# Transposing DMAs in one chain, and queries and keys loaded between the output weights

## The chip, the cores and the metric

The kernel runs on one core of a Trainium2 chip. Its time is the device time of one execution in microseconds (us), given as the median of five runs. One execution is also recorded by the hardware profiler; its page and its trace are what this document reads. Five engines work side by side, each through its own list of instructions in order: TensorE (PE; its weight loads are shown as PEld), VectorE (DVE), ScalarE (ACT), GpSimd (POOL) and SyncE (SP). Here POOL does little but issue the loads, and SP issues the transposing DMAs and the stores. The data of all of them move through the same 16 DMA engines.

## What is computed

An attention whose weights are squared ReLUs, not a softmax, and behind it a gated feed-forward block. There are 8 batches, 12 heads, 448 positions and a head dimension of 64; the block goes from 768 to 1536 and back to 768.

```python
def _attn_ref(q, k, v):
    S = q.shape[2]
    scale = 1.0 / np.sqrt(q.shape[-1])
    scores = scale * np.matmul(q, k.transpose(0, 1, 3, 2))
    attn = np.maximum(scores, 0.0) ** 2 / S
    return np.matmul(attn, v).astype(np.float32)

def _moe_ref(x, w_gate, w_val, w_out):
    g = x @ w_gate
    gelu = 0.5 * g * (1.0 + erf(g * inv_sqrt2))
    val = x @ w_val
    return (gelu * val @ w_out).astype(np.float32)
```

The output of the attention, with its heads laid side by side, is the `x` of the block. Inputs and output are float32 in DRAM; the loads convert to bfloat16.

## The kernel before

**Work of one batch.** Queries and keys of a batch are loaded into one tile `qk16` (queries in the lower 64 partitions, keys in the upper), values into `v16`. For the scores, queries and keys must be transposed into `qkT`. For the first two batches TensorE does this against an identity matrix (L342), and DVE copies the result (L346). From batch 2 on (the third) it is done by DMA: DVE rearranges one group of four heads into `qkr` (L258), and SP issues two transposing DMAs for the group (L262), one for four of its seven chunks of positions and one for the other three. There are three such groups `m` in a batch, so six transposing DMAs. Then come, all over the length of the batch, 21 units of scores (`sp`, TensorE), ReLU (`rl`, ACT, L389) and square (`attnT`, DVE, L395), the six pairs of heads of the values product, whose results DVE copies to `xT` (L448), the gate and value products for 12 columns of the block with Gelu (ACT, L498) and the product `uT` (DVE, L503), and the output tiles (`osb`, ACT copy, L555), which SP stores (L560). All matmuls go through one helper, hence L159.

**Order.** The attention of batch b+1 is interleaved with the block of batch b on TensorE. A planner (`run_plan`, L23) sets the order of every engine's instructions when the program is built. Each piece of work is an `Op` with a cost, other pieces that it waits for and a lag. The lists `PE0` (matmuls on the lower rows) and `POOL` stay in the order in which they were written; from the lists `PE1`, `ACT`, `DVE`, `SP` and `IDLE` the planner takes what can start first, looking at the first 48 pieces. `IDLE` is no engine, only a delay. What the planner settles is an order: on the chip each engine follows its own list and waits by semaphores. For loads the planner keeps a running sum of bytes divided by a rate, and takes a load to have landed 2.0 planned us after its turn in that sum. In the first 30 planned us it also fills gaps of TensorE with matmuls on a tile of zeros (`fill`).

**Loads.** POOL issues them in the order in which they are written (from L581): batch 0, then batch 1 among the gate and value weights `wg` and `wv`, then the four parts of the output weights `wo` (`load_wo`, each 384 of its 1536 rows), then queries and keys of batch 2 in three groups of four heads, then batch 2's values. Loads of batches 3 and later are issued as the block of the batch two before proceeds. Output tile t needs all of `wo`, in order of its rows.

**Transposing DMAs.** `add_dma_transposes` (L248) writes down the delay, the copy and the two transposing DMAs of one group. `EARLY` is 2. For batches after it the second DMA of a group waits on SP for the first to have landed, through the list `one` and a manual dependency; the three groups do not wait for one another. Batch 2 has no such wait: its six DMAs are issued as their copies are done. Batch 2's three groups are written down when the main loop reaches batch 2's first scores (L662); those of later batches when their keys' load is written down.

Of the kernel before, what the change touches and what calls it, by code (L numbers as in the profile page):

```python
# [88 lines left out]
def kernel(  # L89
# [16 lines left out]
    B, H, S, D = q.shape  # L106
    P = 64
    SC = S // P
    VC = (SC + 1) // 2
    NPAIR = H // 2  # L110
    NM = NPAIR // 2
# [13 lines left out]
    EARLY = 2  # L125
# [30 lines left out]
    SYNC = mybir.DependencyInfo(mybir.DependencyClass.Sync, mybir.DependencyReason.DATA)  # L156
# [17 lines left out]
    w12_op, wo_op, head_op = {}, {}, {}  # L174
    qk16, v16 = {}, {}

    def load(nbytes, emit, deps=(), cost=0.7, rate=400e3):
        def paced():
            ins = emit()
            for d in deps:  # L180
                tc.add_manual_dep(ins.ins, d.ins.name, SYNC, reason="pace")

        op = Op("POOL", cost, paced, deps)
        arrivals[op] = nbytes / rate
        POOL.append(op)
        return op

    def load_w12(i):
        cols = slice(i * WCH, (i + 1) * WCH)

        def emit(wt, src):
            return nc.gpsimd.dma_start(
                wt[:, :, :], src[:, cols].rearrange("(c p) f -> p c f", p=128))
        w12_op[i] = [load(4 * d_model * WCH, lambda wt=wt, src=src: emit(wt, src))
                     for wt, src in ((wg[i], moe_w_gate), (wv[i], moe_w_val))]

    def load_wo(i):
        rows = slice(i * WOG * 128, (i + 1) * WOG * 128)
        wo_op[i] = load(4 * WOG * 128 * d_model, lambda: nc.gpsimd.dma_start(
            wo[i][:, :, :], moe_w_out[rows, :].rearrange("(c p) f -> p c f", p=128)))  # L200

    def load_qk(b, i, h0, h1, deps=()):

        src = (q, k)[i]

        def tile_of():
            if b not in qk16:
                qk16[b] = qkv.tile([128, H * S // P * D], bf16, name="qk16", tag="qk16")
            return qk16[b][HALF[i], :]

        op = load(4 * (h1 - h0) * S * D, lambda: nc.gpsimd.dma_start(  # L211
            tile_of().rearrange("p (h x) -> p h x", h=H)[:, h0:h1, :],
            src[b, h0:h1].rearrange("h (p c) d -> p h (c d)", c=SC)), deps, rate=400e3 if b else 300e3)
        for pr in range(h0 // 2, h1 // 2):
            head_op[b, pr, i] = op

    def load_v(b, h0, h1, deps=()):

        for i in range(2):
            def emit(i=i):  # L220
                if b not in v16:
                    v16[b] = qkv.tile([128, H, VC, D], bf16, name="v16", tag="v16")
                c0 = i * (SC - VC)
                return nc.gpsimd.dma_start(  # L224
                    v16[b][HALF[i], h0:h1, :, :],
                    v[b, h0:h1].rearrange("h (p c) d -> p h c d", c=SC)[:, :, c0:c0 + VC, :])
            op = load(4 * (h1 - h0) * VC * P * D, emit, deps, rate=400e3 if b else 300e3)
            for pr in range(h0 // 2, h1 // 2):
                head_op[b, pr, 2 + i] = op

    def load_heads(b, h0, h1):
        load_qk(b, 0, h0, h1)
        load_qk(b, 1, h0, h1)
        load_v(b, h0, h1)

    qkT, tr_op = {}, {}

    def qkT_tile(b):
        if b not in qkT:
            qkT[b] = tpool.tile([128, NM * SC * 2, 2 * P], bf16, name="qkT", tag="qkT")  # L240
        return qkT[b]

    def by_group(t):
        return t.rearrange("d (m c r) x -> d m c r x", m=NM, c=SC)

    qkr = {}

    def add_dma_transposes(b, m):  # L248


        wait = Op("IDLE", 2.0 if b == EARLY else 5.0, lambda: None,
                  [head_op[b, pr, i] for pr in (2 * m, 2 * m + 1) for i in range(2)])
        IDLE.append(wait)

        def emit_copy():
            if b not in qkr:
                qkr[b] = lpool.tile([128, NM, SC, 4, D], bf16, name="qkr", tag="qkr")
            nc.vector.tensor_copy(  # L258
                qkr[b][:, m], qk16[b].rearrange("p (h c d) -> p c h d", c=SC, d=D)[:, :, 4 * m:4 * m + 4])

        def emit_transpose(c0, c1):
            ins = nc.sync.dma_start_transpose(  # L262
                by_group(qkT_tile(b))[:, m, c0:c1].rearrange("d c r x -> d (c r) x"),
                qkr[b][:, m, c0:c1].rearrange("p c h d -> p (c h d)"))
            if b > EARLY:

                if c0:
                    tc.add_manual_dep(ins.ins, one[0].ins.name, SYNC, reason="pace")
                one[:] = [ins]

        one = []
        copy = Op("DVE", 0.65, emit_copy, [wait, *tr_op.get((b - 1, m), ())], lag=0.15, prio=3)
        DVE.append(copy)
        tr_op[b, m] = [Op("SP", 0.19 * 2 * (c1 - c0), lambda c0=c0, c1=c1: emit_transpose(c0, c1),
                          [copy, last_s.get(b - 2)], lag=4.5) for c0, c1 in ((0, VC), (VC, SC))]
        if b > EARLY:
            tr_op[b, m][1].deps.append(tr_op[b, m][0])
        SP.extend(tr_op[b, m])


# [199 lines left out]
    def add_gate_value(at, b, fc, g):  # L480
# [28 lines left out]
        if g == 0:  # L509
            done = gel_op[b, fc] = Op("ACT", 0.55, emit_gelu, [ops[1][-1]], lag=0.06, prio=0)  # L510
            ACT.append(done)
        else:
            done = u_op[b, fc] = Op("DVE", 0.54, emit_mult, [gel_op[b, fc], ops[1][-1]],
                                    lag=0.2, prio=0)
            DVE.append(done)
            if b + 2 < B and b:
                if fc % 2 == 0:
                    m, i = divmod(fc // 2, 2)
                    load_qk(b + 2, i, 4 * m, 4 * m + 4, [done])
                    if i:  # L520
                        add_dma_transposes(b + 2, m)
                elif fc > 6:
                    h0 = 2 * (fc - 7)
                    load_v(b + 2, h0, h0 + 4, [done])
# [56 lines left out]
    for h0, h1 in ((0, 2), (2, 4), (4, 8), (8, 12)):  # L581
        load_qk(0, 0, h0, h1)
        load_qk(0, 1, h0, h1)
        if h0 == 0:
            POOL.append(Op("POOL", 0.6, lambda: make_identity(nc, ident)))
        if h0 > 2:
            load_v(0, h0 - 4, h1 - 4)
# [12 lines left out]
    load_w12(4)  # L600
    load_w12(5)
    for i in range(FC // WOG):
        load_wo(i)
    for m in range(NM):
        for i in range(2):
            load_qk(2, i, 4 * m, 4 * m + 4)
    load_v(2, 0, H)
# [51 lines left out]


    for at, _, fn, args in work:
        if fn is add_scores and args == (2, 0):  # L662
            for m in range(NM):
                add_dma_transposes(2, m)
        fn(at, *args)
# [75 lines left out]
```

## Time and profile before

| | us |
|---|---|
| median of 5 runs | 429.5 (428.2 to 431.69) |
| the profiled execution | 431.69 |
| its span, first to last instruction | 429.8 |
| TensorE busy | 420.8 (98%) |
| TensorE weight loads busy | 359.6 (84%) |
| ScalarE busy | 223.7 (52%) |
| VectorE busy | 212.8 (49%) |
| GpSimd busy | 71.5 (17%) |

The mean granted clock of TensorE is 0.993 of full speed. The page cuts the span into 40 equal slices and gives, for each, the busy share of an engine in tenths, with 9 for 90% and more; the DMA row is the mean busy share of the 16 DMA engines in the same way:

```profile
PE   8999999799999999999999999999999999999996
DVE  2876665157644566355643566455643555212201
ACT  4956662176666555555546555555546555322220
PEclk9999999899999999999999999999999999999998
DMA  7999999977984389544975359845884100120034
```

A slice is 10.7 us. A busy TensorE is not TensorE at its peak, because matmuls overlap one another and their ends are modelled; the number of matmuls in a stretch and the granted clock say more. In lists of waits, "issue" is time for which the profile shows nothing that the engine waited for. A line of the timeline has the start in us, the duration of the merged group, the engine, the source line, the operation, what it writes and reads, how many there are, and in brackets the idle time before it.

The DMAs of the stretch around the change, with issue and landing as the trace has them, in us from the start of the span:

| DMA | issued | landed |
|---|---|---|
| `wo`, four parts | 42.90, 45.73, 46.49, 47.24 | 56.76, 59.56, 62.33, 65.14 |
| batch 2, group 0, queries and keys | 48.49, 50.21 | 66.34, 67.45 |
| group 1 | 52.18, 54.17 | 68.54, 69.70 |
| group 2 | 57.05, 59.84 | 71.21, 72.08 |
| batch 2, values | 62.86, 65.43 | 74.06, 78.31 |
| transposing DMAs, group 0 | 69.88, 74.05 | 78.76, 80.34 |
| stores of the first output tile | 72.84, 73.42 | 79.28, 79.75 |
| transposing DMAs, group 1 | 75.44, 78.59 | 82.62, 83.25 |
| transposing DMAs, group 2 | 83.31, 84.66 | 86.93, 91.62 |

The three copies to `qkr` before the transposing DMAs start at 68.72, 73.54 and 74.6 and take 1.08 us each. The first scores of batch 2 start at 84.8.

### The profile page before, as it was taken

The page shows a single profiled execution, that of the slowest core. Times are in us where ns is not written, and L with a number is a line of the kernel's source. Part 1 is how long each engine was busy: PE and PEld are TensorE (multiplying, and loading weights), DVE is VectorE, ACT ScalarE, POOL GpSimd, SP SyncE. Part 2 cuts the span into 40 slices and gives each one's busy share as a digit, 9 for nine tenths or more (in the row PEclk, how much of TensorE's full clock was granted, in tenths as well). Part 3 has the DMA queues.
Part 4 walks back from the last instruction along what each step waited for, and adds up shares of the span by engine and source line. Part 5 has one row for each costly group of instructions (what it writes and reads, how often), then busy time and mean ns, then how long its engine had stood idle before and what let it go on. Part 6 is the DMA issues. An engine that isn't in the chain of part 4 may idle for free.

```text
span 429.8 us, 19589 instructions
## 1 busy us (share of the span) xinstructions
PE 420.8 (98%) x9087; PEld 359.6 (84%) x9090; DVE 212.8 (49%) x347; ACT 223.7 (52%) x320; POOL 71.5 (17%) x116
## 2 busy tenths in 40 slices
PE   8999999799999999999999999999999999999996
PEld 3558768579998888979999978979999988977895
DVE  2876665157644566355643566455643555212201
ACT  4956662176666555555546555555546555322220
POOL 8655420012200122011300023011310000000000
PEclk9999999899999999999999999999999999999998
DMA  7999999977984389544975359845884100120034
GB/s 99 193 199 197 201 209 193 169 77 97 135 122 93 39 104 135 127 82 69 137 109 118 60 72 150 127 80 58 122 148 103 38 4 3 40 76 2 3 76 113
DMA packets 75217, 44.91 MB, mean 104 GB/s; under 512 B 36096, under 2 KB 71680, under 8 KB 75136
## 3 DMA queue, kind: packets, MB, share of 16 engines
q0 software_dynamic: 37088, 24.39, 42.5%
q1 hardware_dynamic: 37888, 19.08, 25.2%
q8 instruction: 71, 1.16, 1.2%
q10 hardware_dynamic: 160, 0.20, 0.1%
q14 instruction: 10, 0.08, 0.1%
HBM read 48.76 MB, written 11.01 MB: 139 GB/s over the span
## 4 chain that ended last, share of the span: by engine, by line
PE 97%; issue 1%; ACT 1%; DVE 0%
PE ff L159 86%; PE sp L159 8%; PE ff L705 1%; PE ff L304 1%; PE ff L342 1%; PE sp L342 1%; ACT rl L389 1%; DVE qkT L346 0%; DVE attnT L395 0%; DVE osb L555 0%; DVE warm L145 0%; DVE table L148 0%
## 5 line engine op out<-in xcount | busy, mean ns | idle before, releaser
L159 PE MATMUL ff<-xT,wg 64*64 64x448 bf16 x2304 | 217.0, 352 | 0.0
L159 PE MATMUL ff<-xT,wv 64*64 64x448 bf16 x2304 | 215.6, 350 | 0.0
L389 ACT ACTIVATE rl<-sp 128x896 bf16<-128x896 f32 x168 | 152.3, 918 | 96.1 <-PE sp L159 78.4
L159 PE MATMUL ff<-wo,uT 64*64 64x384 bf16 (+1 forms) x2736 | 151.7, 320 | 2.7 <-issue 2.5
L159 PEld LDWEIGHTS <-wv 64*64 64x64 bf16 x2304 | 125.2, 107 | 16.7 <-issue 1.3
L159 PEld LDWEIGHTS <-wg 64*64 64x64 bf16 x2304 | 124.9, 107 | 16.6 <-issue 0.5
L395 DVE TENSOR_TENSOR attnT<-rl 128x896 bf16<-128x896 bf16 x168 | 103.8, 622 | 69.8 <-ACT rl L389 68.6
L159 PEld LDWEIGHTS <-uT 64*64 64x64 bf16 x2736 | 126.2, 107 | 8.8 <-issue 3.8
L159 PE MATMUL sp<-qkT 64*64 64x448 bf16 (+1 forms) x768 | 108.7, 328 | 0.8 <-ACT rl L389 0.5
L503 DVE TENSOR_TENSOR uT<-gel,ff 128x448 bf16<-128x448 bf16 x96 | 59.5, 619 | 82.0 <-PE ff L159 73.1
L159 PE MATMUL ff<-attnT,v 64*64 64x448 bf16 (+1 forms) x768 | 86.1, 326 | 0.1
L498 ACT ACTIVATE gel<-ff 128x448 bf16<-128x448 f32 x96 | 52.1, 543 | 52.1 <-PE ff L159 51.1
L159 PEld LDWEIGHTS <-qkT 64*64 64x64 bf16 x768 | 43.6, 106 | 10.0 <-issue 3.3
L555 ACT COPY osb<-ff 128x384 f32<-128x384 f32 x54 | 25.7, 476 | 49.8 <-PE ff L159 47.1
L159 PEld LDWEIGHTS <-v 64*64 64x64 bf16 x768 | 45.8, 107 | 5.6 <-issue 1.2
L448 DVE TENSOR_SCALAR xT<-ff 128x448 bf16<-128x448 f32 x48 | 29.9, 623 | 33.4 <-PE ff L159 33.4
L211 POOL DMA_DIRECT2D qk<-in_q_dram x25 | 15.6, 622 | 130.5 <-DVE uT L503 123.7
L224 POOL DMA_DIRECT2D v<-in_v_dram x44 | 27.3, 628 | 42.8 <-DVE uT L503 32.0
L211 POOL DMA_DIRECT2D qk<-in_k_dram x25 | 15.4, 615 | 63.5 <-DVE uT L503 55.6
L258 DVE COPY qkr<-qk 128x1792 bf16<-128x1792 bf16 x18 | 19.3, 1078 | 0.0
L555 DVE COPY osb<-ff 128x192 f32<-128x192 f32 (+1 forms) x3 | 1.2, 420 | 18.3 <-PE ff L159 18.3
L342 PEld LDWEIGHTS <-qk 128*64 128x64 bf16 x168 | 5.5, 115 | 2.9 <-issue 2.9
(23 smaller groups left out, 42.6 us busy)
## 6 DMA issues: line engine op xcount, KB each, us to landing
out_dram<-osb SPq DMA_DIRECT2D x54, 192.0 KB, 2.7
v<-in_v_dram POOLq DMA_DIRECT2D x42, 128.0 KB, 4.8
qk<-in_q_dram POOLq DMA_DIRECT2D x23, 224.0 KB, 4.3
qk<-in_k_dram POOLq DMA_DIRECT2D x23, 224.0 KB, 5.1
wg<-in_moe_w_gate_dram POOLq DMA_DIRECT2D x6, 384.0 KB, 10.7
wv<-in_moe_w_val_dram POOLq DMA_DIRECT2D x6, 384.0 KB, 11.8
wo<-in_moe_w_out_dram POOLq DMA_DIRECT2D x4, 576.0 KB, 14.9
v<-in_v_dram POOLq DMA_DIRECT2D x2, 384.0 KB, 12.0
```

Source lines behind the costliest of these rows:

```text
L159: return nc.tensor.matmul(o, lhsT, rhs, start=start, stop=stop, tile_position=(P * row, P * col))
L211: op = load(4 * (h1 - h0) * S * D, lambda: nc.gpsimd.dma_start(tile_of().rearrange("p (h x) -> p h x", h=H)[:, h0:h1, :], src[b, h0:h1].re ...
L224: return nc.gpsimd.dma_start(v16[b][HALF[i], h0:h1, :, :], v[b, h0:h1].rearrange("h (p c) d -> p h c d", c=SC)[:, :, c0:c0 + VC, :])
L258: nc.vector.tensor_copy(qkr[b][:, m], qk16[b].rearrange("p (h c d) -> p c h d", c=SC, d=D)[:, :, 4 * m:4 * m + 4])
L304: nc.tensor.matmul(t[:, :], warm[:, 0:128], warm[:, :], start=True, stop=True)
L342: nc.tensor.transpose(t[HALF[j], c, :], src[:, 2 * (2 * m + r) + j, c, :], ident[:, :], tile_position=(0, P * j))
L389: nc.scalar.activation(rl[:, :, :], box[0][:, :, 0:S], AF.Relu)
L395: nc.vector.tensor_tensor(a[:, :, :], box[1][:, :, :], box[1][:, :, :], op=ALU.mult)
L448: nc.vector.tensor_scalar_mul(xT[b][:, pr, :], box[0][:, 0:S], scalar1=out_scale)
L498: nc.scalar.activation(gel[b, fc][:, :], box[0][:, 0:S], AF.Gelu)
L503: u_op[b, fc].ins = nc.vector.tensor_tensor(uT[b][:, fc, :], gel.pop((b, fc))[:, :], box[0][:, 0:S], op=ALU.mult).ins
L555: (nc.vector.tensor_copy if last else nc.scalar.copy)(osb[t][:, cols], box[0][:, 0:N])
```

## The change

There are four edits, in one step.

1. The rate by which the planner counts loads goes from 400e3 to 425e3 bytes per us, for all loads but those of batch 0's queries, keys and values, which keep 300e3. This alters no load, only the planned times and with them the order in which the planner puts instructions.
2. Every transposing DMA waits for the one before it to have landed, over all groups and batches; in the planner each has the one before among what it waits for.
3. The loads of queries and keys of batch 2's first group stand between the second and the third part of `wo`; the other two groups stay behind the fourth.
4. The copies and transposing DMAs of batch 2 are written down when the main loop comes to batch 1's first gate product, no longer at batch 2's first scores.

```diff
-    def load(nbytes, emit, deps=(), cost=0.7, rate=400e3):
+    def load(nbytes, emit, deps=(), cost=0.7, rate=425e3):
...
-            src[b, h0:h1].rearrange("h (p c) d -> p h (c d)", c=SC)), deps, rate=400e3 if b else 300e3)
+            src[b, h0:h1].rearrange("h (p c) d -> p h (c d)", c=SC)), deps, rate=425e3 if b else 300e3)
...
-            op = load(4 * (h1 - h0) * VC * P * D, emit, deps, rate=400e3 if b else 300e3)
+            op = load(4 * (h1 - h0) * VC * P * D, emit, deps, rate=425e3 if b else 300e3)
...
-    qkr = {}
+    qkr, one, turn = {}, [], []
...
-            if b > EARLY:
-
-                if c0:
-                    tc.add_manual_dep(ins.ins, one[0].ins.name, SYNC, reason="pace")
-                one[:] = [ins]
-
-        one = []
+
+            if one:
+                tc.add_manual_dep(ins.ins, one[0].ins.name, SYNC, reason="pace")
+            one[:] = [ins]
+
...
-        if b > EARLY:
-            tr_op[b, m][1].deps.append(tr_op[b, m][0])
+        for op in tr_op[b, m]:
+            op.deps.extend(turn)
+            turn[:] = [op]
...
     for i in range(FC // WOG):
+        if i == 2:
+            load_qk(2, 0, 0, 4)
+            load_qk(2, 1, 0, 4)
         load_wo(i)
-    for m in range(NM):
+    for m in range(1, NM):
         for i in range(2):
             load_qk(2, i, 4 * m, 4 * m + 4)
...
-        if fn is add_scores and args == (2, 0):
+        if fn is add_gate_value and args == (1, 0, 0):
             for m in range(NM):
                 add_dma_transposes(2, m)
```

## The prediction

> **What bounds the kernel now.** I read four views in turn: the chain of waits, the table of stretches, the order of time around the one stretch that is odd, and the DMA queues.
>
> The chain of waits puts the whole span on TensorE, nearly all of it on matmuls (L159):
>
> ```profile
> PE 97%; issue 1%; ACT 1%; DVE 0%
> ```
>
> So only time in which TensorE stands still, or runs at a lower clock, can be gained. The waits of TensorE name one such place, with no releaser:
>
> ```profile
> PE ff L159 <- issue: 2.5, 1, 2.5
> ```
>
> The table of stretches, one microsecond a row, shows where it is (PE busy, PEld, DVE, ACT, POOL, then granted clock, DMA share, GB/s):
>
> ```profile
> 75.00:76.00 1.00, 1.00 (x30) 0.84 (x24) 0.61 (x1) 0.43 (x1) 0.00 (x0) 1.00 1.39 131
> 76.00:77.00 1.00, 0.40 (x10) 0.00 (x0) 0.00 (x0) 0.00 (x0) 0.00 (x0) 1.00 2.37 107
> 77.00:78.00 1.00, 0.00 (x0) 0.00 (x0) 0.00 (x0) 0.00 (x0) 0.00 (x0) 1.00 0.21 14
> 78.00:79.00 1.00, 0.07 (x4) 0.08 (x8) 0.00 (x0) 0.00 (x0) 0.00 (x0) 0.90 0.81 320
> 79.00:80.00 1.00, 1.00 (x14) 0.63 (x18) 0.00 (x0) 0.00 (x0) 0.00 (x0) 0.50 1.18 262
> 80.00:81.00 1.00, 1.00 (x16) 0.85 (x12) 0.00 (x0) 0.00 (x0) 0.00 (x0) 0.50 1.31 298
> 81.00:82.00 1.00, 1.00 (x16) 0.82 (x9) 0.00 (x0) 0.42 (x1) 0.00 (x0) 0.50 1.50 47
> 82.00:83.00 1.00, 1.00 (x24) 0.71 (x21) 0.00 (x0) 0.60 (x2) 0.00 (x0) 0.90 0.33 65
> ```
>
> Every engine stops together, DMA falls to 14 GB/s, and TensorE then works at a clock of 0.50. The order of time shows what goes on beside it:
>
> ```profile
> 74.05 5.92 SPq L262 DMA_TRANSPOSE qkT<-qkr  x3
> ...
> 76.07 0.33 PE L159 MATMUL ff<-wo,uT 64*64 64x384 bf16 x2
> 78.92 0.12 PEld L159 LDWEIGHTS <-uT 64*64 64x64 bf16 x2 [2.93 <-issue]
> 78.92 0.53 PE L159 MATMUL ff<-wo,uT 64*64 64x384 bf16 x2 [2.53 <-issue]
> ```
>
> The matmul at 78.92 continues an output tile whose inputs were all there, so what was missing is the instruction itself. The queues have a row for that:
>
> ```profile
> q8 instruction: 71, 1.16, 1.2%
> ```
>
> 71 packets of 16,384 bytes against TensorE's 18,195 instructions are 256 to a packet. Counted in 256s, TensorE stops at instruction 10.74, and the small gap before 64.89 stands at 8.74, exactly two packets earlier: both are packet borders. In the trace's packet records the fetches between 38 and 69 start 3.3 to 3.8 us after the border that precedes them, take 0.9 to 1.0 and end 1.3 to 1.6 before the next border; 256 instructions last some 6 us. The fetch of 75.05 started 4.2 us after its border, took 2.40 and ended at 77.45, past the border; work resumed 1.47 later. So an end some 1.3 to 1.5 before the border is just in time, and the fetches before it had no more than 0.3 to spare. From 92 on most start within 1 us of the border (2.5 at most) and leave 3 to 5: the load queue no longer fills the DMA engines, of which it alone moved 204 GB/s between 40 and 70. My reading is that a transposing DMA under full loads delayed a fetch that had no slack.
>
> **What the change costs and gains, step by step.** The sum starts from the profiled execution, 431.69 us (span 429.83 and 1.86 around it). It is the slowest of the five; the median is 429.5.
>
> *The stall that may go.* 2.53 us idle, then 3.3 us at half clock (78.9 to 82.2), which lose 1.65. Together 4.2. The actions and copies after it run 4.3 us later against the kernel's own plan than those before it, which agrees. If no fetch meets a transpose any more: minus 4.2. If one still does, 0.
>
> The Trainium skill, Runtime: NRT & Kernel Launch, section Instruction fetch mechanics, says that crossing a 16 KiB border is mostly hidden because dispatch is slower than the refill; by that nothing here is to be gained and the sum would stay at 431.7. The idle 2.53 us on a border is against it. The page TensorE: Matmul & The Clock Gate, section on the HAM clock gate, has the clock drop after an idle window of about 3.4 us; here 2.53 us of idle was enough for 0.50, so the measurement decides. By the page only 2.53 would be gained.
>
> *The reordered loads.* The first queries and keys of the third batch took 1.20 and 1.11 us of the full queue (landings 65.14, 66.34, 67.45). Moved ahead of wo2 and wo3 (the third and fourth part) they land at about 60.7 and 61.9, and wo2 and wo3 2.31 later, at 64.64 and 67.45. The first output tile reaches wo3's rows at about 67.2. That is a wait of 0.3 us; at the least 0, and 0.9 if transposes already hold the engines. I take 0.3, since the transposes' first packets come at about 66.8 (below). All POOL issues stay the same in number (each waits for the one eight before it, as 57.05 does for the landing at 56.76), and the last two value loads still land long before batch 2's values at 95.0.
>
> *The earlier copies.* The new rate makes the plan expect loads earlier. The loads counted at 400e3 before and 425e3 after, the first copy (L258) becomes due 8.4 us earlier in the plan, the other two 3.0 and 3.1. DVE runs in order, so the copy goes to about 62.7, before the multiply at 63.69, ahead of which DVE was idle 0.95; its 1.08 us fit but for 0.1, which TensorE doesn't see. Its data have landed by 61.9. Without that cover DVE would hold the multiplies and squares behind it, 1 us at most. The second copy now stands ahead of the copy of xT at 73.00 (before which DVE idled 3.21), with its keys at 69.70; cover again, until that landing slips past 72.
>
> *The chain.* Each transposing DMA now waits on SP for the one before; behind it wait only the stores of the first output tiles, whose buffers are four deep. Six in a row from about 63.8, at 4.7 us median to landing and 8.9 at most, end by 92 to 100. Batch 2's first scores ran at 84.8 and need two of the six, the third and fourth some 12 us later: hidden at 4.7 each (73), and hidden at 8.9 each by 3 us (81.6). For later batches pairs were already chained, and a neighbour's pair had landed.
>
> *Fetches in the new place.* The first transpose was issued at 69.88 and moved its first packets at 73.0 under full loads; from 63.8 that is 66.8 to 70. The fetch of 68.55 falls inside. The nearest row of one transpose beside loads is the fetch of 87.72: 1.96 instead of 0.95, thus +1.0; the ends are 0 (missed) and 4.2 (the stall before with its clock). The next fetch, near 75, meets the second transpose or the 3 us gap that the chain leaves between landing and next packets: 0 to 4.2 too. I take 1.0 once, for one of the two, with no loss of clock.
>
> Sum: 431.69 - 4.2 + 0.3 + 1.0 = 428.8. This is 0.7 under the median of 429.5, or 0.2%.
>
> **Rivals.**
>
> *The stall goes altogether.* For it: the chain leaves at most one transpose in flight, and the stores between two transposes no longer pile up (store packets of 3072 bytes took up to 1.9 us at 76.3). Against it: the fetch of 75.05 began late when only the first transpose moved data. If the stall costs each run alike, the time is 429.5 - 4.2 + 0.3 = 425.6.
>
> *More fetches stall (slower).* Transposes now overlap full loads from 66.8 to beyond 80 rather than from 73 to 77, so both the fetch of 68.55 and the one near 75 can starve TensorE. It decides as soon as each is later than its slack of 0.3 us. One as before (4.2) and one at 1.5: 431.69 - 4.2 + 0.3 + 5.7 = 433.5. Against it: with transposes in flight after 90 no fetch took over 1.8.
>
> *One stall trades for one stall.* The second fetch or the first simply takes the place of the old one with its clock loss or without: 430.0 to 431.7, no change to speak of. The chain then doesn't do what it says, since a single transpose is enough.
>
> **How the numbers follow.** Short waits in place of the stall 0.32 (own range 427.3 to 430.8); stall gone 0.28; more stalls 0.28; one for one 0.12. Differences within 0.5% (427.4 to 431.6) are about what this kernel's measurement can't tell from no change. Faster: the 0.28 less a tenth, plus an edge of the likeliest, 0.31. Slower: the 0.28 and an edge of the last, 0.30. The rest, 0.39, is the same. The range takes in 425.5, just under the stall gone, and 433.5.
>
> **What would show it.** In the profile after: the row "issue" of TensorE's waits at 2.5 or gone, and where; the granted clock between 64 and 90 below 1.00 or not; the first copy at about 62.7 and the first transposing DMA at 63.8; a wait for wo at 67; transposes one at a time, the last landing by 100. I am wrong if the stall isn't the fetch, if batch 2's scores wait for the chain, or if DVE held by an early copy stops TensorE.

## The result and the profile after

The changed kernel takes 429.68 us, the median of 43 executions (428.78 to 435.56). The kernel before takes 428.2 us, the median of 80 executions (427.0 to 432.24). The ratio is 1.0031, interval 1.0022 to 1.0041: 0.3%, or 1.3 us, slower. That lies inside the 0.5% called no change in the prediction, but the forecast had the sign the other way.

The page of the changed kernel (execution of 429.82 us, span 428.0) shows the clock, the DMA share and the chain of waits:

```profile
PEclk9999999999999999999999999999999999999998
DMA  8999999999985399545975379635983100120034
PE 81%; DMA 15%; POOL 2%; issue 1%; DVE 0%; DVEq 0%; ACT 0%; POOLq 0%
```

The chain was nearly all TensorE before. Now it leaves TensorE for DMAs at two places. One is the last two transposing DMAs of batch 2 (89.28 to 96.14, 1.6% of the span), ahead of which it is on TensorE again. The other is the wait for `wo` at 67.5, and from there it goes into the loads of the start, most of the 15%. That share is no measure of the loss: a kernel below that has no wait at the first place still shows 14%. The places are what to look for, and the waits of TensorE name three candidates (releaser, total, times, longest):

```profile
PE ff L159 <- DMA wo<-in_moe_w_out_dram: 1.0, 1, 1.0
PE ff L159 <- DVE xT L447: 0.9, 1, 0.9
PE ff L159 <- issue: 0.7, 1, 0.7
```

The old wait of 2.5 without a releaser has become three waits of about 1 us with three different causes. The order of time of TensorE places them:

```profile
67.58 0.35 PE L159 MATMUL ff<-wo,uT 64*64 64x384 bf16 x2 [0.95 <-DMA wo<-in_moe_w_out_dram]
...
77.34 0.35 PE L159 MATMUL ff<-wo,uT 64*64 64x384 bf16 x2 [0.68 <-issue]
...
98.12 0.57 PE L159 MATMUL ff<-xT,wg 64*64 64x448 bf16 x6 [0.92 <-DVE xT L447]
```

The first is the fourth part of `wo`, which landed at 67.54. The second stands at instruction 10.74 counted in packets of 256, the same packet border as before. The third is new and far from the loads that were moved. VectorE's order of time shows where it comes from:

```profile
62.17 1.08 DVE L258 COPY qkr<-qk 128x1792 bf16<-128x1792 bf16 x1
...
71.96 1.09 DVE L258 COPY qkr<-qk 128x1792 bf16<-128x1792 bf16 x1 [2.85 <-DMA qk<-in_k_dram]
73.10 0.62 DVE L447 TENSOR_SCALAR xT<-ff 128x448 bf16<-128x448 f32 x1
75.05 1.09 DVE L258 COPY qkr<-qk 128x1792 bf16<-128x1792 bf16 x1 [1.32 <-DMA qk<-in_k_dram]
...
96.45 1.09 DVE L258 COPY qkr<-qk 128x1792 bf16<-128x1792 bf16 x1 [2.08 <-DMA qkT<-qkr]
97.46 0.61 DVE L447 TENSOR_SCALAR xT<-ff 128x448 bf16<-128x448 f32 x1
```

The first three copies are batch 2's, at the places that were forecast. The fourth, at 96.45, is batch 3's first. It writes `qkr`, of which there is one buffer (`lpool`, one tile), so it must wait until batch 2's last transposing DMA has read it; that landed at 96.14. Behind the copy on VectorE stands the copy of `xT`, and TensorE waits for that.

The DMAs of the stretch, in us from the start of the span:

| DMA | issued | landed |
|---|---|---|
| `wo`, four parts | | 56.84, 59.88, 64.74, 67.54 |
| batch 2, group 0, queries and keys | | 60.74, 61.88 |
| groups 1 and 2, keys | | 71.87, 74.96 |
| batch 2, values | 61.27, 62.17 | 77.34, 79.10 |
| transposing DMAs, one to three | 63.34, 74.90, 79.98 | 74.89, 79.90, 83.70 |
| transposing DMAs, four to six | 83.71, 89.28, 92.73 | 89.22, 92.71, 96.14 |

### The profile page after: what moved, and what is told of

It reads as the page before. It is cut to its first block, busy times and chain, and to the rows that moved or that the text cites. A ratio compares the mean times of both kernels' runs of the same rounds, so it can differ in the third digit from the quotient of the medians.

```text
span 428.0 us, 19588 instructions
## 1 busy us (share of the span) xinstructions
PE 419.0 (98%) x9087; PEld 358.2 (84%) x9090; DVE 213.1 (50%) x347; ACT 223.7 (52%) x320; POOL 71.5 (17%) x116
## 4 chain that ended last, share of the span: by engine, by line
PE 81%; DMA 15%; POOL 2%; issue 1%; DVE 0%; DVEq 0%; ACT 0%; POOLq 0%
PE ff L159 75%; PE sp L159 6%; DMA wv<-in_moe_w_val_dram 5%; DMA qk<-in_k_dram 4%; DMA wo<-in_moe_w_out_dram 4%; DMA qkT<-qkr 2%; POOL qk L211 1%; POOL v L224 0%; POOL wg L192 0%; DVE xT L447 0%; DVE osb L554 0%; POOL ident masks.py:199 0%; POOL ident masks.py:197 0%; DVEq L258 0%; DVE qkr L258 0%
## 5 line engine op out<-in xcount | busy, mean ns | idle before, releaser
L211 POOL DMA_DIRECT2D qk<-in_k_dram x25 | 15.4, 615 | 66.6 <-DVE uT L502 57.8
```

## The experiments

All ratios are to the kernel before, timed on the same chip in the same rounds.

**What the old pause costs, and what the planner's rate does alone.** The profiled execution of before (431.69 us) was far above the median, so I took another, unchanged.

> The kernel before, unchanged, for a profile of an ordinary execution, since the one recorded (431.69 us) was far above the median of 428.2. Theory (the recorded one was one of the rare executions in which the pause at the packet border was long enough to lower the clock): the pause near 76 us is 0.3 to 1.5 us, the granted clock stays at 1.00, span about 426.5. Rival (every execution has the pause of 2.5 us and the half clock): span about 429.8 with a clock of 0.50 behind 78 us.

It ran in 428.27 us, span 426.5. Its waits of TensorE:

```profile
PE ff L159 <- issue: 1.2, 1, 1.2
```

The pause is there, at the same packet border (75.70 to 77.17 from the start of one matmul to the start of the next), but it is 1.2 us and not 2.5, and the granted clock stayed at 1.00 behind it. The fetch began 4.32 us after its border and took 0.92. Of the 80 executions of the kernel before, 73 took 429.6 us or less and seven 431.08 or more, none between. The one that the prediction was worked from is of the seven. Another 93 executions of this kernel were timed beside the experiments, each with its mean granted clock: nine took 430.7 us or more, and eight of these had a clock of 0.993 to 0.996, all the others 0.997 or more. So a long execution is as a rule one that lost its clock.

Then edit 1 by itself:

```diff
-    def load(nbytes, emit, deps=(), cost=0.7, rate=400e3):
+    def load(nbytes, emit, deps=(), cost=0.7, rate=425e3):
...
-            src[b, h0:h1].rearrange("h (p c) d -> p h (c d)", c=SC)), deps, rate=400e3 if b else 300e3)
+            src[b, h0:h1].rearrange("h (p c) d -> p h (c d)", c=SC)), deps, rate=425e3 if b else 300e3)
...
-            op = load(4 * (h1 - h0) * VC * P * D, emit, deps, rate=400e3 if b else 300e3)
+            op = load(4 * (h1 - h0) * VC * P * D, emit, deps, rate=425e3 if b else 300e3)
```

> Only the rate of 425e3, nothing else of the change. It puts the copy of batch 3's first group ahead of the xT copy on VectorE, as the changed kernel has it, but the transposes of batch 2 aren't chained. Theory (the order alone is harmless, it needs the late chain): no wait for xT near 97 us, ratio 0.998 to 1.001. Rival (the reordered plan itself costs the time): ratio 1.003 and the wait for xT of about 0.9 us.

Ratio 1.0004 (0.9983 to 1.0025). The pause is 0.9 us. Batch 3's first copy to `qkr` now stands ahead of a copy of `xT` on VectorE. The kernel before, in its ordinary execution:

```profile
94.62 0.62 DVE L448 TENSOR_SCALAR xT<-ff 128x448 bf16<-128x448 f32 x1 [0.41 <-PE ff L159]
95.16 1.08 DVE L258 COPY qkr<-qk 128x1792 bf16<-128x1792 bf16 x1
```

and with the new rate alone:

```profile
93.43 1.08 DVE L258 COPY qkr<-qk 128x1792 bf16<-128x1792 bf16 x1
94.43 0.62 DVE L448 TENSOR_SCALAR xT<-ff 128x448 bf16<-128x448 f32 x1
```

Without the chain nothing holds the copy (batch 2's last transposing DMA landed at 89.45) and TensorE has no wait there. So this edit sets the order, and alone it costs nothing.

**Is the wait for `xT` the loss?** Two kernels take it away in different ways. One gives `qkr` a second buffer:

```diff
-    lpool = ctx.enter_context(tc.tile_pool(name="lpool", bufs=1))
+    lpool = ctx.enter_context(tc.tile_pool(name="lpool", bufs=2))
```

> The changed kernel with two buffers for qkr, so that batch 3's first copy doesn't wait for batch 2's last transpose. Theory (the chain ends at 96.1 us and the copy, which stands ahead of xT's on VectorE, waits for it): the wait for xT of 0.9 us near 97 goes, the waits for wo (1.0) and at the packet border (0.7) stay; some 1.2 us less than the changed kernel, ratio to the kernel before about 1.0005 (0.999 to 1.002). Rival (xT's wait only takes the place of another): ratio 1.003 as the changed kernel's.

Ratio 0.9985 (0.996 to 1.001). VectorE at the place in question:

```profile
94.62 1.08 DVE L258 COPY qkr<-qk 128x1792 bf16<-128x1792 bf16 x1
95.62 0.62 DVE L447 TENSOR_SCALAR xT<-ff 128x448 bf16<-128x448 f32 x1
```

Same order, but no bracket with idle time: the copy has its own buffer. In this stretch TensorE's waits that are left are 1.0 without a releaser and 0.4 for `wo`.

The other keeps one buffer and changes a delay of the planner just enough that the two copies change places on VectorE:

```diff
-        wait = Op("IDLE", 2.0 if b == EARLY else 5.0, lambda: None,
+        wait = Op("IDLE", 2.0 if b == EARLY else 5.1, lambda: None,
```

> The changed kernel with a planned delay of 5.1 in place of 5.0 for batches after the third; on VectorE this exchanges one pair of neighbours, so that the xT copy of batch 2's first pair of heads stands ahead of batch 3's first copy to qkr again; one qkr buffer as changed. Theory (the chain is late, but it hurts only because xT's copy stands behind the copy that waits): the wait for xT of 0.9 us goes, ratio 0.998 to 1.001, as with two buffers. Rival (the late copy holds VectorE's next multiply just as well): half of the loss or more stays, ratio 1.0015 to 1.003.

Ratio 0.9998 (0.9977 to 1.0019).

```profile
94.15 0.62 DVE L447 TENSOR_SCALAR xT<-ff 128x448 bf16<-128x448 f32 x1 [0.41 <-PE ff L159]
95.59 1.08 DVE L258 COPY qkr<-qk 128x1792 bf16<-128x1792 bf16 x1 [0.81 <-DMA qkT<-qkr]
```

The copy to `qkr` still waits for the chain's end, which landed at 95.27, and nobody behind it is in need. The intervals of both kernels end below the point where that of the change begins (1.0022). Their medians, 428.36 and 428.42, are 1.3 us under that of the change and within 0.3 of the kernel before beside them (428.26 and 428.17). In the profiled executions the wait for `wo` is shorter as well (0.4 and 0.3, not 1.0), but that is not it. From the first matmul behind this wait to the end of the span the change takes 360.4 us and both of these 359.4, although their pause at the packet border is 0.3 longer (1.30 and 1.38 from start to start, not 1.03). What is left is the wait for `xT`, 1.27 from start to start. So the loss comes of two edits that meet, the order that edit 1 makes and the late chain of edit 2, on a buffer that neither edit mentions.

**The chain by itself, and the change without it.** Edits 2 and 4 on the kernel before:

```diff
+            if one:
+                tc.add_manual_dep(ins.ins, one[0].ins.name, SYNC, reason="pace")
+            one[:] = [ins]
...
+        for op in tr_op[b, m]:
+            op.deps.extend(turn)
+            turn[:] = [op]
...
-        if fn is add_scores and args == (2, 0):
+        if fn is add_gate_value and args == (1, 0, 0):
```

> The kernel before with the chain alone (and the earlier place in the program that it needs); TensorE, VectorE, ScalarE and GpSimd keep their order of instructions, only SyncE's waits change. Theory (the chain's end holds the copy into the single qkr buffer): the first transpose is issued near 69.5 as before, six at 5 us or so end at 98 to 102, batch 3's first copy, due near 98, waits 1 to 4 us and VectorE with it; TensorE then waits 0.5 to 3 us near 99 to 102; ratio 1.002 to 1.008. Rival (the chain is harmless, the reordered copies are what costs): ratio 1.000, no wait near 100.

Ratio 1.0103 (1.0068 to 1.0138). The largest wait of TensorE is not at `xT`:

```profile
PE sp L159 <- DMA qkT<-qkr: 2.7, 1, 2.7
```

TensorE stood from 82.25 to 85.29 for batch 2's first scores, and 3.41 us at clock 0.50 followed. All lists but SP's are in the order of the kernel before; on SP the two stores of the second output tile (issued at 79.35 and 79.86) come ahead of the second transposing DMA. It was issued at 80.50, 2.3 us after the first had landed, and landed at 85.25. The copy to `qkr` waited 0.97 behind a copy of `xT`, which is harmless. The loss is above the 1.002 to 1.008 that was expected, and its place is another.

The change without edit 2, in the plan and on the chip:

```diff
-            if one:
-                tc.add_manual_dep(ins.ins, one[0].ins.name, SYNC, reason="pace")
-            one[:] = [ins]
+            if b > EARLY:
+                if c0:
+                    tc.add_manual_dep(ins.ins, one[0].ins.name, SYNC, reason="pace")
+                one[:] = [ins]
...
-        for op in tr_op[b, m]:
-            op.deps.extend(turn)
-            turn[:] = [op]
+        if b > EARLY:
+            tr_op[b, m][1].deps.append(tr_op[b, m][0])
```

> The changed kernel without the chain: rate and order of loads as changed, batch 2's six transposes as free as before. Theory (the chain is what makes batch 2's transposes end late): the last lands before 92 us, no wait for xT, the wait for wo of about 1 us stays; ratio 0.999 to 1.002. Rival (the chain is what keeps the pause at the packet border short): a pause of 2 us or more between 64 and 80 with the half clock, ratio 1.006 or more.

Ratio 1.0127 (1.0105 to 1.015), and it answers another question than the one asked:

```profile
PE sp L159 <- DMA qkT<-qkr: 4.2, 1, 4.2
```

Freed from the chain's planned lateness, the planner put the first scores of batch 2 some 125 matmuls earlier into TensorE's list, and on the chip their transposes came late (TensorE stood from 74.37 to 78.97, with 6.83 us at clock 0.50 after it). The chain in the plan is thus also what keeps those scores where their data can be. To leave all orders alone, the next kernel keeps the chain in the plan and drops the waits of batch 2's transposing DMAs on the chip. As the edit is written, later batches lose the waits between their groups too, and only the pair within a group stays chained. In the trace one later DMA made use of that (issued at 171.72, with the one before landing at 172.41), and TensorE has no gap over 0.5 us after 85:

```diff
-            if one:
-                tc.add_manual_dep(ins.ins, one[0].ins.name, SYNC, reason="pace")
-            one[:] = [ins]
+            if b > EARLY:
+                if c0:
+                    tc.add_manual_dep(ins.ins, one[0].ins.name, SYNC, reason="pace")
+                one[:] = [ins]
```

> The changed kernel with the chain left in the plan but not on the chip: every engine's order of instructions is that of the changed kernel, only the waits of batch 2's transposes for one another are off. Theory (the late chain alone makes the wait for xT): batch 2's last transpose lands before 91, batch 3's first copy doesn't wait, no wait for xT near 97; the wait for wo (0.3 to 1.0) and a pause at the border near 76 stay; ratio 0.998 to 1.001. Rival (the first transposes, now free to pile up under full loads, delay a fetch by 2.5 us and cost the clock): ratio 1.005 or more.

Ratio 1.0021 (1.0006 to 1.0035), between the two accounts. The wait for `xT` is gone, since batch 2's transposes end at 90.65. In its place:

```profile
PE ff L159 <- issue: 1.2, 2, 0.7
```

Two pauses, both on packet borders (76.38 to 77.47 and 83.64 to 84.49). The fetches before them started 3.74 and 3.83 us after their borders and took 1.39 and 1.90. With the chain the fetch that serves the second border started 2.81 us after its own and took 1.07, and there was no pause at 84. So in these two executions the chain does protect fetches, by about one short pause; what it gains there it lost at `qkr`.

**Where the pause near 76 comes from, and a version without it.** Back to the old order of loads, with rate, chain and two buffers:

```diff
-        if i == 2:
-            load_qk(2, 0, 0, 4)
-            load_qk(2, 1, 0, 4)
...
-    for m in range(1, NM):
+    for m in range(NM):
```

> Two qkr buffers and the chain and the rate, but the old order of loads (first queries and keys of batch 2 behind all output weights). Theory: the wait for wo (0.4 to 1.0 us at 67) goes; the pause at the packet border near 76 stays at 0.9 to 1.5, since transposes and loads still meet there; ratio 0.995 to 0.999, about 0.5 us less than with two buffers alone. Rival (TensorE is held by the fetch anyway, and the wait for wo was hidden in front of it): the same time as with two buffers alone, and a longer pause at the border.

Ratio 0.9995 (0.9972 to 1.0018), not to be told from the same kernel with the new loads (0.9985). The wait for `wo` is gone, 0.4 us by the row of the other kernel, and the time does not show it. The profiled execution (430.67 us, the highest of its twelve; their median is 428.2) waits 2.0 us at the border near 76, and its clock falls to 0.50 for 3.41 us. A wait at `wo` stands some 9 us ahead of that border; my reading, which no run isolates, is that it lets the loads run ahead of TensorE and is taken off the pause that follows.

Next I took the load out of the way. Batch 2's values, two DMAs of 384 KB that nobody needs before 95, are issued only after batch 1's first product `uT`; this is on the kernel before, without any edit of the change:

```diff
+            if (b, fc) == (1, 0):
+                load_v(2, 0, H, [done])
...
-    load_v(2, 0, H)
```

> The kernel before with batch 2's values loaded only when batch 1's first product of the block is done (near 81 us instead of 63 to 78); all engines' orders of instructions but GpSimd's as before. Theory (the pause needs the transposes and a full load queue together): the loads end by 73, the fetch near 74 starts within 2 us of its border, no pause near 76; 1.2 us less, ratio 0.996 to 0.998. Rival (the transposes alone delay the fetch): a pause of 1 us or more stays, ratio 1.000.

Ratio 0.9985 (0.996 to 1.0009); the profiled execution took 427.4 us. From 23 us to the end of the span TensorE has no gap over 0.5 us from start to start. The fetch before the border began 2.01 us after its own, not 4.32, and ended 2.33 ahead of the next. The mechanism is as supposed. The gain in time, 0.15% by the ratio and 0.06% by the medians (427.91 against 428.17), is smaller than the pause of 1.2 us (0.28%); the interval takes in that and nothing as well, so what the pause is worth in time is not shown.

With rate, chain, two buffers and old loads as well:

> Chain, rate, two qkr buffers, the old order of loads, and batch 2's values loaded near 81: every wait seen so far taken away and the chain kept. Theory (the chain itself is worth nothing where the loads don't meet the transposes): no pause at 76, no wait for wo or xT, the same time as late values alone, ratio 0.996 to 0.999. Rival A (the chain is worth something of its own): 0.5 us or more below late values alone. Rival B (the chain of six, started near 69, ends too late for something else): a new wait of TensorE between 84 and 105.

Ratio 0.9979 (0.9962 to 0.9997), median 427.02 us: faster than both kernels compared here, though not to be told from the late values alone. This is its page's chain and the largest wait of TensorE, which is at the start of the program:

```profile
PE 99%; ACT 0%; DVE 0%; issue 0%
```

```profile
PE ff L705 <- DVE table L148: 1.2, 1, 1.2
```

Batch 2's chain of DMAs ends at 99.70, later than in the changed kernel (96.14), and costs nothing, because batch 3's first copy, at 92.30, has the other buffer.

Two further kernels vary this one, which their expectations call e9. The first has the change with the exchanged copies (the delay of 5.1, called e5), late values and again one buffer:

> The changed kernel with xT's copy ahead of batch 3's first copy (as in e5) and with batch 2's values loaded near 81. Theory: the first transpose still meets full loads from 63 to 74, so the fetch near 74 stays just in time, but the pause shrinks from 1.0 to at most 0.5; the wait for wo of 0.3 to 1.0 us stays; ratio 0.997 to 1.000, no better than late values alone. Rival (the waits for wo and at the border add up as before): ratio 1.000 to 1.001.

Ratio 1.0115 (1.0076 to 1.0154). Neither account foresaw it. VectorE's order of time:

```profile
94.22 0.62 DVE L447 TENSOR_SCALAR xT<-ff 128x448 bf16<-128x448 f32 x1 [0.41 <-PE ff L159]
99.47 1.09 DVE L258 COPY qkr<-qk 128x1792 bf16<-128x1792 bf16 x1 [4.62 <-DMA qkT<-qkr]
100.47 0.61 DVE L502 TENSOR_TENSOR uT<-gel,ff 128x448 bf16<-128x448 bf16 x1
```

The late values now run beside the middle of the chain: the fourth transposing DMA was issued at 81.60 and landed at 91.64, and the last landed at 99.16. The copy of `xT` is safe in front, but the copy to `qkr` waits 4.6 us, and now it is the product `uT` behind it that TensorE needs: it stood from 97.61 to 101.14, and 6.83 us at clock 0.50 followed. It is the wait of the changed kernel in a larger dose. Exchanging the two copies had only moved the danger to the next instruction in line.

The other is the fastest version, but with batch 2's transposing DMAs free of one another on the chip, by the same edit as in the kernel with the waits off:

> As e9 (rate, two qkr buffers, old order of loads, batch 2's values near 81), with the chain left in the plan but batch 2's transposes free of one another on the chip: all engines keep e9's order. Theory (without full loads beside the transposes the chain is worth nothing): no pause near 76, no wait of TensorE between 60 and 105 over 0.5, ratio 0.996 to 0.999 as e9's 0.998. Rival (the chain gives e9 its gain over late values alone): 0.5 us or more slower than e9, a pause at the border of 0.5 us or more.

Ratio 1.0045 (1.0024 to 1.0066). The interval is apart from that of the fastest version, so here the chain's waits are worth 0.7%: the theory failed. The rival had the time right and not the place, for there is no pause at the border. VectorE, of an execution that was the fastest of the twelve (428.68 us; the median is 430.17):

```profile
95.34 1.08 DVE L258 COPY qkr<-qk 128x1792 bf16<-128x1792 bf16 x1 [2.86 <-DMA qk<-in_k_dram]
96.34 0.61 DVE L448 TENSOR_SCALAR xT<-ff 128x448 bf16<-128x448 f32 x1
```

The same copy is late again, with two buffers, and this time for its data. TensorE waits 1.4 us for `xT`. The loads of batch 3's first queries and keys were issued at 80.89 and 84.32 in this kernel and at 80.79 and 84.23 in the fastest, but landed at 93.98 and 95.25, not 89.59 and 90.98. The stretches of 92 to 94 (PE, PEld, DVE, ACT, POOL, clock, DMA share, GB/s) in this kernel:

```profile
92.00:94.00 2.00, 1.99 (x45) 1.54 (x40) 0.48 (x1) 1.27 (x2) 0.00 (x0) 1.00 1.52 89
```

and in the fastest:

```profile
92.00:94.00 2.00, 2.00 (x50) 1.78 (x46) 1.91 (x3) 1.37 (x2) 0.00 (x0) 1.00 0.62 103
```

In the one the fifth and sixth transposing DMAs (issued at 81.46 and 84.41, landed at 95.24 and 97.49) are in flight beside these loads, and the engines are held 1.52 of 2 us for 89 GB/s; in the other only the fifth is, from 91.94, and they are held 0.62 for 103. The kernel with late values alone, whose transposing DMAs are just as free, has the same late landings, 94.17 and 95.30, and no loss, since its copy of `xT` is not behind the copy to `qkr`. So my reading is that the chain leaves room for the loads beside it. As the profiled execution is 1.5 us below the median, its 1.4 us may be less than what most executions wait.

## Why the prediction came out as it did

The time, 429.68, is inside the range; the direction is not as forecast. Part of that lies in what the sum was compared with: 428.8 is above the 428.2 of 80 executions, and it read as faster because two of the five behind the median of 429.5 were long ones (431.22 and 431.69). That the number came near owes something to two errors that are one and the same pause: the start of the sum was 3.4 above an ordinary execution (431.69 against 428.27), and the stall taken off it was 3.0 too large.

**The step that failed** is the chain, "Batch 2's first scores ran at 84.8 and need two of the six, the third and fourth some 12 us later: hidden". That is right for the scores: they did not wait in the changed kernel. But I followed the transposing DMAs only to the readers of what they write. They also read `qkr`, and the next writer of `qkr` is a copy on VectorE, an engine that works in order. That they "end by 92 to 100" was right (96.14), though the upper end is not what its row gives: six at 8.9 from 63.8 end at 117.2, and the third and fourth at 99.4, later than the scores that need them, 12 us after 84.8. The late end alone should have led to the question who needs it. In the same way I gave the rate edit's effect on batch 2's copies and left out batch 3's first copy, which the edit put ahead of `xT`. Cost: 0.9 us of waiting (1.27 from start to start; 1.3 by the medians), shown by the two kernels that remove it in two ways.

**The stall that may go** was sized 4.2 from an execution that few others resemble. The mechanism was right, in its place as well: fetch, full load queue, packet border. But it is 1.2 us in the ordinary execution, with no loss of clock, and the change took only 0.5 of it away (0.7 left; 1.0 in the profiled executions with two buffers and with exchanged copies). That the full load queue is needed is shown by the late values; the part of the transposing DMA is argued, since no run keeps the loads and takes it away. The prediction noted that its execution was 2.2 above the median and did not draw the consequence that a stall of just that size may be what sets it apart.

**The reordered loads**: the landings were right within 0.1 us (60.74, 61.88, 64.74 and 67.54 against 60.7, 61.9, 64.64 and 67.45). The wait was 0.95, not 0.3; the upper end given, 0.9, was the one to take, since TensorE arrived at wo3's rows at 66.6 and not 67.2.

**The earlier copies**: the first at 62.17 (62.7), followed by the multiply at 63.20; the second at 71.96, with its keys landed at 71.87, just inside the cover until 72. No cost, as said.

**Fetches in the new place**: 1.0 for one wait; it was 0.7, at the fetch near 75 and not that of 68, which took 0.94.

Made from the ordinary execution, the sum is 428.27 - 1.2 + 0.95 + 0.9 + 0.7 = 429.6, against 429.82 profiled. With the right size of the stall and my other terms it would have been 428.27 - 1.2 + 0.3 + 1.0 = 428.4, no change. The missing 0.9 and the 0.65 by which the wait for `wo` was short, less the 0.3 by which the fetch was long, make the difference.

**The cases.** Short waits in place of the stall is what happened, and 429.68 is inside that case's own range; but there are three of them, and one was not in the sum. The stall did not go altogether, nor did it trade one for one. More stalled fetches did not come with the chain, but they did where its waits were left out. Open is why some executions of the kernel before lose the clock, the profiled one after a pause of 2.5 us at the border, and others pause 1.2 and keep it: nothing that was varied here picks the one or the other.

## What to carry to other kernels

When transfers are made to wait for one another, look for whoever needs the last of them, and count the next writer of the buffers they read among these; if that writer sits on an in-order engine, so does everything behind it. A new order of instructions is to be checked against the landings that the same change brings, since here each alone was harmless at this place. Before a stall is priced, compare its execution with the median: one that is 1% above may owe that to the very stall.

## What the runs showed of the hardware

**A transposing DMA beside full loads.** In the changed kernel the first was issued at 63.34 and landed at 74.89, 11.6 us, while 131 to 206 GB/s were moved in the four stretches of 3 us from 63 to 75; the median of all 36 is 3.8. The fourth one beside late values took 10.0 (81.60 to 91.64). The Trainium skill, Advanced Engine Details and Errata, section X-Bar Transpose (TRN2), has transposing DMAs as fast as regular ones. No run here compares the two alone, and the loads issued in the changed kernel between 42 and 63 took 13.9 to 18.4 to land. But beside a full load queue the median of 4.7 that the prediction took was 2.5 times too short, and its highest row, 8.9, was too short as well.

**When TensorE loses its clock.** Gaps of 1.28, 1.48 and 1.73 us from start to start left the granted clock at 1.00 (the changed kernel, the kernel before, the late values with free transposing DMAs). Gaps of 2.30 (two buffers, old loads), 2.85 (the execution that the prediction shows) and 3.04 (the chain alone) were followed by about 3.4 us at 0.50, those of 3.52 (exchanged copies, late values) and 4.60 (no chain) by 6.83. The page TensorE: Matmul & The Clock Gate, section on the HAM clock gate, puts the drop after an idle window of about 3.4 us; here a gap of 2.30 was enough and one of 1.73 was not. In all these traces the granted clock changes only at whole multiples of 3.41 us after its first rise. The two gaps that cost 6.83 ran on 1.5 and 1.1 us past the drop (77.44 to 78.97, 100.01 to 101.14), the other three 0.1 or not at all. How a gap between 1.73 and 2.30 counts, no run shows.

**Instruction fetches under load.** In the fastest version the fetches of TensorE's packets between 37 and 69 start 3.2 to 3.8 us after their borders and take 0.9 to 1.0, where a packet lasts 5.8 to 6.1: they end 1.3 to 1.7 before they are needed. In the four kernels with late values the next one started 2.0 to 2.7 after its border, against 4.32 in the kernel before, and none of the four paused at the border near 76.
